# Moving a weight prefetch in time and in memory: three more weight tiles in the space of the raw inputs, most of them behind the last q/k/v loads, and hand-ordered first and last attention units

## The chip, the cores and the metric

The kernel runs on one core of one Trainium2 chip; the other cores do nothing. The engines go by their names in the profile: PE multiplies matrices (PEld loads its weights), DVE, ACT and POOL are the vector, scalar and GpSimd engines, SP issues the loads. "Products" are matmuls; acc is the PSUM buffer that takes those with a weight tile. The "DMA share" is the mean busy share of the core's 16 DMA engines; in short windows it reads a little above 1, so values near 1 mean full. The metric is the device time of one launch in microseconds. Two kernels are compared on the same chip in alternating rounds. "Span" is the time from the first to the last instruction of a profiled run; it is some 1.7 us shorter than the time of that run.

## The reference, cut to what matters

```python
# attention: 8 batches, 8 heads, 576 tokens, head dim 64
scores = q @ k^T / 8 + ALiBi bias; keys 0..127 tokens back only
x = softmax(scores) @ v                       # -> [8, 576, 512]
# spectral mixing
X = rfft(x, axis=1)[:, :64]                   # 64 modes
Y = X * (w_r + i w_i)                         # per mode a complex 512 x 512 matrix
u = x + irfft(Y)
out = u + relu(u @ w_ch)
```

The inputs q, k and v have 28.3 MB together. The weights w_r and w_i have 128 matrices of 512 x 512 in fp32, each 1.0486 MB: 134.2 MB. They are read once and nothing of them is used twice. The tolerance allows bf16 products.

## The kernel before

The kernel has three stages. Attention runs in 16 units (a batch and four heads), the weights stream past PE as tiles of 1 MB, and a tail of inverse transforms, ReLU and stores follows. The order of work on every engine is fixed by hand in this kernel. SP issues every load, also in a fixed order.

A cast frees a raw input buffer and at once asks for the load two units ahead:

```python
    def cast(self, u, w):
        src = self.loaded.pop((w, u))
        ...                                   # DVE casts to bf16
        self.load(w, u + 2)                   # raw pool: two buffers each of q, k, v
```

A weight tile is asked for every second stage, into a pool of eight buffers (`NW = 8`), among which is the one that first holds w_ch:

```python
        for stage in range(min(lags), n + max(lags)):          # n = 16 units
            for name, arg, lag in STAGE:                        # the software pipeline
                u = stage - lag
                if 0 <= u < n:
                    getattr(at, name)(u, arg)
            if stage > 0 and (stage % 2 == 1 or stage == n - 2):
                load_w()                                        # first call: w_ch
            if stage == 12:
                nc.gpsimd.tensor_copy(wch, wq[0])
```

In the weight stage every step uses one tile and asks for the next one. A load must wait until PE has used the tile whose buffer it takes:

```python
        for g in range(NM // 4):
            for i in range(8):
                w = wq[1 + 2 * m + ri]
                for a in range(4):
                    nc.tensor.matmul(acc[...], lhsT=XC[...], rhs=w[:, a]...)
                load_w()
                ...                           # side work: x @ w_ch, transposes
```

XC holds the spectra of all 16 units, so the first of these products needs the last unit of attention. Its last steps are two value products into one PSUM buffer (`av`), two norms on DVE, the spectrum on PE (`xt`) and its copy to XC by ACT.

The softmax here doesn't subtract the row's maximum and nothing guards it: scores larger than these inputs give would overflow.

## Time and profile before

| | before |
|---|---|
| median of the runs | 492.09 us before the change was run, 491.88 with one run more |
| profiled run | 487.15 us, span 485.5 us |
| DMA queue empty | about 128.5 to 139.5 us |
| first weight product (acc) | 137.0 us |
| last weight landed | about 439.7 us |
| last weight product to the end | 43.1 us |

The first fence shows four rows of the page of the kernel before: the span in 40 slices of 12.1 us, with busy tenths of PE and DVE, the DMA engines, and what they moved.

```profile
PE   1777767658579676675575667668678686688994
DVE  6599898989852101011011010211111201002885
...
DMA  8999999999549999999999999999999999992677
GB/s 252 315 285 269 320 286 327 291 288 259 234 171 423 421 421 420 422 422 420 421 422 422 421 423 421 421 421 421 422 419 423 423 421 420 422 422 98 241 277 263
```

Attention fills the first eleven slices, at about 285 GB/s on average. From slice 13 to 36 the weights stream at 421 GB/s, so that a tile takes 1.0486 MB / 421 GB/s = 2.49 us. PE is busy for two thirds of that time. The slices of 5 and 4 tenths, the eleventh and twelfth, are the thing to see: in about half of each DMA has nothing to do.

The next fence has the windows view of the kernel before. Columns: window, its length, then busy time and instructions of PE, PEld, DVE, ACT and POOL, granted clock, DMA share, GB/s.

```profile
120.00:124.00 4.00, 2.67 (x50) 1.87 (x48) 3.93 (x10) 4.00 (x6) 0.00 (x0) 1.00 0.88 343
124.00:128.00 4.00, 2.66 (x64) 2.29 (x61) 3.86 (x9) 3.70 (x6) 0.00 (x0) 1.00 1.01 424
128.00:132.00 4.00, 2.03 (x31) 1.64 (x32) 2.42 (x5) 0.00 (x0) 0.00 (x0) 0.61 0.04 14
132.00:136.00 4.00, 2.83 (x30) 2.40 (x27) 2.42 (x15) 0.00 (x0) 1.50 (x9) 0.50 0.00 0
136.00:140.00 4.00, 3.04 (x13) 1.21 (x12) 3.75 (x5) 0.87 (x2) 0.00 (x0) 0.50 0.07 8
```

Why it has nothing to do is seen in the timeline of SP, which issues the loads. These two lines follow each other:

```profile
119.89 0.38 SPq L386 DMA_DIRECT2D w<-in_moe_w_i_dram  x1
138.91 0.33 SPq L386 DMA_DIRECT2D w<-in_moe_w_r_dram  x1
```

All eight buffers are spoken for at 119.9 us, and their data is there at 128.5. The next load is issued at 138.9, when PE has used the first tile. From then on DMA never stops until the last weight has landed. The chain of waits shows this as long pieces of one kind (start, length, what):

```profile
168.80 18.74 DMA w<-in_moe_w_i_dram
187.58 1.08 PE acc L496 x4
188.68 18.75 DMA w<-in_moe_w_i_dram
```

Each piece is one load in the full queue of eight: 8 x 2.49 = 19.9 us from its issue to its product. So the time of this kernel is: when streaming can resume, plus the tiles still to come times 2.49, plus the tail.

### The profile page before, as it was taken

What the parts mean: (1) busy time and instruction counts of PE and PEld (TensorE: products, weight loads), DVE (VectorE), ACT (ScalarE), POOL (GpSimd) and SP (SyncE); (2) the same over time, 40 slices, a digit from 0 to 9 for tenths busy, and PEclk for the clock granted to TensorE, in tenths of its full rate; (3) what the DMA queues carried; (4) which work ended last, traced back from release to release, by engine and by line L of the source; (5) the groups of instructions that cost most, each with busy time, mean ns of one, the idle gap of its engine ahead of it and who ended that gap; (6) DMA issues with size and microseconds to landing.
All of it is one profiled execution on the core that took longest, in us unless ns stands there. A gap on an engine that the chain in (4) does not pass through costs nothing.

```text
span 485.5 us, 6274 instructions
## 1 busy us (share of the span) xinstructions
PE 339.8 (70%) x2411; PEld 175.5 (36%) x2430; DVE 189.4 (39%) x395; ACT 156.4 (32%) x212; POOL 33.5 (7%) x58
## 2 busy tenths in 40 slices
PE   1777767658579676675575667668678686688994
PEld 1455555546434323232232223323333232223431
DVE  6599898989852101011011010211111201002885
ACT  3897977988531000000000000101010100002674
POOL 6101000000010000000000000000000000000564
PEclk9997987998869989989989999988888978769999
DMA  8999999999549999999999999999999999992677
GB/s 252 315 285 269 320 286 327 291 288 259 234 171 423 421 421 420 422 422 420 421 422 422 421 423 421 421 421 421 422 419 423 423 421 420 422 422 98 241 277 263
DMA packets 71087, 173.44 MB, mean 357 GB/s; under 512 B 41360, under 2 KB 41360, under 8 KB 54672
## 3 DMA queue, kind: packets, MB, share of 16 engines
q1 hardware_dynamic: 71056, 173.03, 94.8%
q8 instruction: 19, 0.31, 0.3%
q14 instruction: 12, 0.10, 0.1%
HBM read 163.58 MB, written 9.44 MB: 356 GB/s over the span
## 4 chain that ended last, share of the span: by engine, by line
DMA 58%; PE 16%; DVE 14%; ACT 4%; issue 4%; SPq 3%; POOL 1%; POOLq 0%; DVEq 0%; ACTq 0%
DMA w<-in_moe_w_i_dram 45%; DMA w<-in_moe_w_r_dram 8%; PE acc L496 6%; DMA kr<-in_k_dram 4%; DVE x L296 3%; DVE att_130 L252 3%; DVE att_131 L252 2%; SPq L178 2%; DVE k L200 2%; DVE q L200 1%; PE av L282 1%; DMA qr<-in_q_dram 1%; PE warm L486 1%; PE mm L540 1%; PE mm L550 1%
## 5 line engine op out<-in xcount | busy, mean ns | idle before, releaser
L496 PE MATMUL acc<-w,XC 128*32 128x512 bf16 x512 | 153.3, 433 | 85.8 <-DMA w<-in_moe_w_r_dram 42.2
L496 PEld LDWEIGHTS <-XC 128*32 128x32 bf16 x512 | 64.7, 137 | 151.8 <-issue 125.8
L481 ACT CAST XW<-my 128x512 bf16<-128x512 f32 x36 | 21.1, 585 | 237.3 <-PE my L479 208.8
L475 DVE COPY xT<-tr 128x512 bf16<-128x512 bf16 x36 | 15.3, 425 | 161.8 <-PE tr L473 161.7
L563 POOL TENSOR_TENSOR r<-r,x 128x512 f32<-128x512 f32 x18 | 20.8, 1157 | 324.6 <-ACT r L560 324.6
L479 PE MATMUL my<-wch,xT 128*128 128x512 bf16 x129 | 38.6, 405 | 2.9 <-DVE xT L475 1.5
L240 ACT ACTIVATE att_130<-sc 128x1024 bf16<-128x1024 f32 x32 | 31.9, 1050 | 2.3 <-PE sc L231 2.2
L240 ACT ACTIVATE att_131<-sc 128x1024 bf16<-128x1024 f32 x32 | 32.1, 1038 | 0.5 <-PE sc L231 0.4
L427 DVE CAST yq<-acc 128x512 bf16<-128x512 f32 x16 | 11.0, 688 | 49.7 <-PE acc L496 49.7
L296 DVE TENSOR_TENSOR x<-av,rec 128x640 bf16<-128x640 f32 x32 | 26.4, 825 | 1.1
L569 DVE TENSOR_TENSOR o<-yy,r 128x512 f32<-128x512 f32 x36 | 23.6, 688 | 6.3 <-ACT r L560 4.3
L560 ACT ACTIVATE r<-mm 128x512 f32<-128x512 f32 x36 | 21.2, 597 | 8.9 <-PE mm L550 4.9
L252 DVE TENSOR_TENSOR att_131<-att_131,mask 128x1024 bf16<-128x1024 bf16 (+2 forms) x40 | 23.4, 618 | 0.0
L282 PEld LDWEIGHTS <-att_131 128*128 128x128 bf16 x288 | 12.9, 109 | 27.9 <-DVE x L296 25.5
L458 ACT CAST Zs<-zw 64x512 bf16<-64x512 f32 x16 | 9.2, 577 | 40.3 <-PE zw L449 40.1
L479 PEld LDWEIGHTS <-xT 128*128 128x128 bf16 x144 | 11.8, 102 | 28.6 <-issue 21.3
L215 ACT COPY qkT_128<-tp 128x1152 bf16<-128x1152 bf16 x15 | 16.8, 1117 | 15.9 <-PE tp L209 15.8
L252 DVE TENSOR_TENSOR att_130<-att_130,mask 128x1024 bf16<-128x1024 bf16 (+2 forms) x40 | 21.7, 576 | 0.3 <-ACT att_130 L240 0.3
L209 PE MATMUL tp<-ident,q 128*128 128x128 bf16 x144 | 14.0, 259 | 11.1 <-DVE q L200 7.8
L459 DVE CAST Zs<-z 64x512 bf16<-64x512 f32 x16 | 11.0, 687 | 22.5 <-PE z L452 22.3
L215 ACT COPY qkT_129<-tp 128x1152 bf16<-128x1152 bf16 x16 | 18.2, 1135 | 1.6 <-PE tp L209 1.6
L315 PE MATMUL xt<-F,x 128*128 128x128 bf16 x160 | 12.7, 246 | 4.7 <-DVE x L296 3.4
(95 smaller groups left out, 339.9 us busy)
## 6 DMA issues: line engine op xcount, KB each, us to landing
w<-in_moe_w_r_dram SPq DMA_DIRECT2D x64, 1024.0 KB, 18.7
w<-in_moe_w_i_dram SPq DMA_DIRECT2D x64, 1024.0 KB, 18.7
qr<-in_q_dram SPq DMA_DIRECT2D x16, 576.0 KB, 5.4
kr<-in_k_dram SPq DMA_DIRECT2D x16, 576.0 KB, 5.0
vr<-in_v_dram SPq DMA_DIRECT2D x64, 128.0 KB, 5.9
out_dram<-o SPq DMA_DIRECT2D x32, 256.0 KB, 2.4
vr<-in_v_dram SPq DMA_DIRECT2D x16, 64.0 KB, 5.2
w<-in_moe_w_ch_dram SPq DMA_DIRECT2D x1, 1024.0 KB, 8.5
```

Source lines behind the costliest of these rows:

```text
L215: (self.nc.vector.tensor_copy if (u, w) == (0, "q") else self.nc.scalar.copy)(dst.rearrange("q h (p j) -> q h p j", j=TPP), tp.rearrange(" ...
L240: self.nc.scalar.activation(self.att[u % 2][:, kt * 8 * P : (kt + 1) * 8 * P], sc.rearrange("p e n -> p (e n)"), AF.Exp, scale=1.0 / math. ...
L252: nc.vector.tensor_tensor(out=heads[:, :, c0 : c0 + n], in0=heads[:, :, c0 : c0 + n], in1=mask[:, :, m0 : m0 + n], op=ALU.mult,)
L282: nc.tensor.matmul(dst, lhsT=lhsT, rhs=vb[:, kt, hv, : D + 1], start=(n == 0), stop=(n == len(terms) - 1),)
L296: nc.vector.tensor_tensor(out=self.x[:, b, :, cs].rearrange("p t (h d) -> p h t d", h=2), in0=tiles[:, :, :, :D], in1=rec.unsqueeze(-1).br ...
L475: nc.vector.tensor_copy(xT, tr)
L479: nc.tensor.matmul(mm, lhsT=xT[:, dt], rhs=wch[:, dt], start=(dt == 0), stop=(dt == 3))
L481: nc.scalar.copy(XW[:, i], mm)
L496: nc.tensor.matmul(acc[32 * (i // 2) : 32 * (i // 2) + 32], lhsT=XC[:, c0 : c0 + 31 * NM + 1 : NM], rhs=w[:, a].bitcast(BF16)[:, 1::2], st ...
L560: nc.scalar.activation(r, mm, AF.Relu)
L563: nc.gpsimd.tensor_tensor(out=r, in0=r, in1=xi, op=ALU.add)
L569: nc.vector.tensor_tensor(out=o, in0=yy, in1=r, op=ALU.add)
```

## The change

Its intent is to give DMA more tiles to load before PE frees the first one, and to end attention earlier.

1. Three extra weight tiles lie in the memory of the raw q/k/v buffers once these are done, so that eleven tiles can be loaded before PE frees one. They are used once; the depth in the stream stays eight.
2. Of the eight ordinary tiles only four are loaded among the q/k/v loads, and four behind them. w_ch comes in two halves through raw q buffers and is copied by ACT instead of POOL.
3. The first units are ordered by hand: loads q0, k0, q1, k1 first, the table of sines in two parts, 24 products to warm PE.
4. In the last unit, the second value product takes another PSUM buffer, and ACT and DVE share the copy of `xt`.
5. Some buffers of the tail (Zs, r, o) move to the memory of the extra tiles.

```diff
-            if stage > 0 and (stage % 2 == 1 or stage == n - 2):
+            if stage in (3, 6, 9, 12):
                 load_w()
-            if stage == 12:
-                nc.gpsimd.tensor_copy(wch, wq[0])
+            if stage == n - 4:
+                halves = [at.raw.tile([P, 2, TPP, D], FP32, tag="qr", name="wch") for _ in "ab"]
+                ...                                        # two DMAs of w_ch
+            if stage in (n - 3, n - 2):
+                load_w(2)
+            if stage == n - 1:
+                for a, t in enumerate(halves):
+                    nc.scalar.copy(wch[:, 2 * a : 2 * a + 2], t.rearrange(...))
+                at.rawctx.close()
+                wpool2 = w2ctx.enter_context(
+                    tc.tile_pool(name="w2", bufs=3, side="right", reuse_waits="tile"))
+                load_w(3, wpool2)
...
-        for w in "qkv":
-            for u in range(2):
-                at.load(w, u)
+        for w, u in (("q", 0), ("k", 0), ("q", 1), ("k", 1), ("v", 0), ("v", 1)):
+            at.load(w, u)
...
+            for _ in range(24):
+                nc.tensor.matmul(wt, lhsT=ident, rhs=ident, start=True, stop=True)
+            run("cast", "q", 0)
+            run("transpose", "q", 0)
...                                                        # and so on for k0, q1, k1
-        av = self.ps.tile([P, 2, 512], FP32, tag="av")
+        last = u == len(self.units) - 1 and e == 1
+        av = self.ps.tile([P, 2, 512], FP32, tag="sc" if last else "av", ...)
...
+            lo, hi = slice(0, 2), slice(2, 4)              # last unit only
+            nc.scalar.copy(view[:, lo, 8 + b : 24 : 8, :], xt[:, 0, lo])
+            nc.vector.tensor_copy(view[:, hi, 8 + b : 24 : 8, :], xt[:, 1, hi])
...
+                if 8 * g + i == 16:
+                    w2ctx.close()
+                    right = mctx.enter_context(tc.tile_pool(name="late", ...))
+                    Zs = right.tile([P, B, 2, DM], BF16, name="Zs")
```

More of the change, by code (lines that the diff above doesn't have):

```diff
@@ L80, in _forward_table @@
         nc.vector.tensor_scalar_add(ang[:, :, ri, :], prod, float(S) / (4 - 2 * ri))
+    yield
     _sin_of(nc, pool, F[:, : FULL + 1].rearrange("p a b -> p (a b)"),
@@ L133, in __init__ @@
         self.units = [(b, g) for b in range(B) for g in range(self.NG)]
-        self.raw = ctx.enter_context(tc.tile_pool(name="raw", bufs=2))
+        self.rawctx = ctx.enter_context(ExitStack())
+        self.raw = self.rawctx.enter_context(tc.tile_pool(name="raw", bufs=2, side="right"))
         self.mid = ctx.enter_context(tc.tile_pool(name="amid", bufs=2))
@@ L206, in transpose @@
         src = self.casted.pop((u, w))
-        tp = self.ps.tile([P, TPP, P], BF16, tag="tp")
+        if (u, w) == (0, "k"):
+            tp = self.ps.tile([P, TPP, P], BF16, tag="sc", bufs=2, name="tp")
+        else:
+            tp = self.ps.tile([P, TPP, P], BF16, tag="tp", name="tp")
         for j in range(TPP):
@@ L214, in evacuate @@
         dst = self.qkT[u % 2][:, "qk".index(w), :, : self.S]
-        (self.nc.vector.tensor_copy if (u, w) == (0, "q") else self.nc.scalar.copy)(
+        (self.nc.vector.tensor_copy if u < 2 and w == "q" else self.nc.scalar.copy)(
             dst.rearrange("q h (p j) -> q h p j", j=TPP),
@@ L263, in value @@
         att, vb = self.att[u % 2], self.vb[u % 3]
-        av = self.ps.tile([P, 2, 512], FP32, tag="av")
+        last = u == len(self.units) - 1 and e == 1
+        av = self.ps.tile([P, 2, 512], FP32, tag="sc" if last else "av", bufs=2 if last else 1)
         for h in range(2):
@@ L311, in spectrum @@
         NM = self.F.shape[2] // 2
-        xt = self.ps.tile([P, 4, 2, NM], FP32, tag="tp")
+        last = u == len(self.units) - 1
+        xt = self.ps.tile([P, 2, 4, 2, NM], FP32, tag="tp")
         for a in range(4):
@@ L315, in spectrum @@
                 nc.tensor.matmul(
-                    xt[:, a].rearrange("p r m -> p (r m)"),
+                    xt[:, a // 2 if last else 0, a].rearrange("p r m -> p (r m)"),
                     lhsT=self.x[:, b, st, a::4],
@@ L331, in channels @@
         view = self.XC[:, : 4 * NC * NM].rearrange("p (a c m) -> p a c m", a=4, c=NC)
-        nc.scalar.copy(view[:, :, 8 + b : 24 : 8, :], xt)
-        nc.scalar.mul(view[:, :, b, :], xt[:, :, 1, :], -1.0)
+        if u < len(self.units) - 1:
+            nc.scalar.copy(view[:, :, 8 + b : 24 : 8, :], xt[:, 0])
+            nc.scalar.mul(view[:, :, b, :], xt[:, 0, :, 1, :], -1.0)
+        else:
+            lo, hi = slice(0, 2), slice(2, 4)
+            nc.scalar.copy(view[:, lo, 8 + b : 24 : 8, :], xt[:, 0, lo])
+            nc.scalar.mul(view[:, lo, b, :], xt[:, 0, lo, 1, :], -1.0)
+            nc.vector.tensor_copy(view[:, hi, 8 + b : 24 : 8, :], xt[:, 1, hi])
+            nc.vector.tensor_scalar_mul(view[:, hi, b, :], xt[:, 1, hi, 1, :], -1.0)
 @with_exitstack
@@ L361, with load_w @@
     wch = const.tile([P, 4, DM], BF16, name="wch")
-    with tc.tile_pool(name="setup", bufs=1) as pool:
-        make_identity(nc, ident)
-        kv_i = pool.tile([P, 2], I32)
-        nc.gpsimd.iota(kv_i, [[-P, 2]], base=0, channel_multiplier=1)
-        kv = pool.tile([P, 2], FP32)
-        nc.vector.tensor_copy(kv, kv_i)
-        _forward_table(nc, pool, F, S)
-        for h in range(H):
-            slope = 2.0 ** (-8.0 * (h + 1) / H)
-            nc.scalar.activation(ek[:, h], kv, AF.Exp, scale=slope)
     wpool = ctx.enter_context(tc.tile_pool(name="w", bufs=NW))
     wq = []
-    def load_w():
-        i = len(wq) - 1
-        if i >= 2 * NM:
-            return
-        t = wpool.tile([P, 4, DM], FP32, tag="w", name="w")
-        if i < 0:
-            src = moe_w_ch.rearrange("(a p) e -> p a e", p=P)
-        else:
+    def load_w(n=1, wpool=wpool):
+        for i in range(len(wq), min(len(wq) + n, 2 * NM)):
+            t = wpool.tile([P, 4, DM], FP32, tag="w", name="w")
             src = (moe_w_r, moe_w_i)[i % 2][i // 2].rearrange("(p a) e -> p a e", a=4)
-        nc.sync.dma_start(out=t, in_=src)
-        wq.append(t)
+            nc.sync.dma_start(out=t, in_=src)
+            wq.append(t)
+    w2ctx = ExitStack()
     with ExitStack() as actx:
@@ L391, with run @@
         n = len(at.units)
-        for w in "qkv":
-            for u in range(2):
-                at.load(w, u)
+        for w, u in (("q", 0), ("k", 0), ("q", 1), ("k", 1), ("v", 0), ("v", 1)):
+            at.load(w, u)
+        done = set()
+        def run(name, arg, u):
+            if 0 <= u < n and (name, arg, u) not in done:
+                done.add((name, arg, u))
+                getattr(at, name)(u, arg)
+        make_identity(nc, ident)
+        with tc.tile_pool(name="setup", bufs=1) as pool:
+            kv_i = pool.tile([P, 2], I32)
+            nc.gpsimd.iota(kv_i, [[-P, 2]], base=0, channel_multiplier=1)
+            kv = pool.tile([P, 2], FP32)
+            nc.vector.tensor_copy(kv, kv_i)
+            table = _forward_table(nc, pool, F, S)
+            next(table)
+            wt = at.ps.tile([P, P], FP32, tag="av", bufs=1, name="warm")
+            for _ in range(24):
+                nc.tensor.matmul(wt, lhsT=ident, rhs=ident, start=True, stop=True)
+            run("cast", "q", 0)
+            run("transpose", "q", 0)
+            next(table, None)
+            run("cast", "k", 0)
+            run("transpose", "k", 0)
+            run("evacuate", "q", 0)
+            run("evacuate", "k", 0)
+            for h in range(H):
+                slope = 2.0 ** (-8.0 * (h + 1) / H)
+                nc.scalar.activation(ek[:, h], kv, AF.Exp, scale=slope)
         at.fixtures()
@@ L398 @@
         nc.gpsimd.memset(XC[:, 4 * NC * NM :], 0.0)
+        for name, arg, u in (("cast", "q", 1), ("cast", "k", 1), ("transpose", "q", 1),
+                             ("evacuate", "q", 1)):
+            run(name, arg, u)
         lags = [lag for _, _, lag in STAGE]
@@ L401 @@
             for name, arg, lag in STAGE:
-                u = stage - lag
-                if 0 <= u < n:
-                    getattr(at, name)(u, arg)
-            if stage > 0 and (stage % 2 == 1 or stage == n - 2):
+                run(name, arg, stage - lag)
+            if stage in (3, 6, 9, 12):
                 load_w()
-            if stage == 12:
-                nc.gpsimd.tensor_copy(wch, wq[0])
+            if stage == n - 4:
+                halves = [at.raw.tile([P, 2, TPP, D], FP32, tag="qr", name="wch") for _ in "ab"]
+                halves = [t.rearrange("p e j d -> p (e j d)")[:, : 2 * DM] for t in halves]
+                for a, t in enumerate(halves):
+                    nc.sync.dma_start(
+                        out=t.rearrange("p (a e) -> p a e", a=2),
+                        in_=moe_w_ch[2 * a * P : 2 * a * P + 2 * P].rearrange(
+                            "(a p) e -> p a e", p=P),
+                    )
+            if stage in (n - 3, n - 2):
+                load_w(2)
+            if stage == n - 1:
+                for a, t in enumerate(halves):
+                    nc.scalar.copy(wch[:, 2 * a : 2 * a + 2], t.rearrange("p (a e) -> p a e", a=2))
+                at.rawctx.close()
+                wpool2 = w2ctx.enter_context(
+                    tc.tile_pool(name="w2", bufs=3, side="right", reuse_waits="tile")
+                )
+                load_w(3, wpool2)
     with ExitStack() as mctx:
@@ L413 @@
         YT = fix.tile([P, 2, 4, B, 2, HM], BF16, name="YT")
-        Zs = fix.tile([P, B, 2, DM], BF16, name="Zs")
         with tc.tile_pool(name="setup2", bufs=1) as pool:
@@ L421 @@
         XW = big.tile([P, 9 * (B // 2), DM], BF16, name="XW")
-        load_w()
         def quad_end(acc, g):
@@ L488 @@
         quads, side, todo = [], [], 0
+        Zs = None
         for g in range(NM // 4):
@@ L492 @@
                 m, ri = 4 * g + i // 2, i % 2
-                w = wq[1 + 2 * m + ri]
+                w = wq[2 * m + ri]
                 for a in range(4):
@@ L503 @@
                 load_w()
+                if 8 * g + i == 16:
+                    w2ctx.close()
+                    right = mctx.enter_context(
+                        tc.tile_pool(name="late", bufs=1, side="right", reuse_waits="tile")
+                    )
+                    Zs = right.tile([P, B, 2, DM], BF16, name="Zs")
                 if quads:
@@ L558, in end @@
             inverse(mm, 0, bs, st, False)
-            r = pool.tile([P, DM], FP32, tag="r", bufs=3)
+            r = right.tile([P, DM], FP32, tag="r", bufs=3, name="r")
             nc.scalar.activation(r, mm, AF.Relu)
@@ L567, in store @@
             xi, bs, st = tiles[i]
-            o = pool.tile([P, DM], FP32, tag="o", bufs=5)
+            o = right.tile([P, DM], FP32, tag="o", bufs=5)
             nc.vector.tensor_tensor(out=o, in0=yy, in1=r, op=ALU.add)
```

## The prediction

> **What bounds the kernel now.** (1) Attention, 0 to 134 us: windows give DVE 3.9 us busy of most 4 us and a DMA share of 0.9 to 1.15, so both are near their limit, at only about 285 GB/s, because v arrives in 256 B runs (the Trainium skill, "DMA: Bandwidth & Descriptors", Specifications, puts line rate at 512 B or more; the trace agrees: 421 in the weight stage). (2) Weight streaming, 139.5 to 440 us: DMA share 1.01 at 421 GB/s throughout, PE busy two thirds; the chain of waits is almost only "DMA w". A tile of 1.0486 MB takes 2.49 us. (3) Tail, 45 us. Total time is when streaming resumes, plus the tiles left times 2.49, plus the tail.
>
> Before streaming lies a hole: windows show a DMA share of 0.09, 0.00, 0.00, 0.13 from 128 to 140 us. All eight weight buffers are full at 128.5, and PE frees the first at 138.9: 11 us.
>
> **What the change does.**
> - Three extra weight tiles in the raw inputs' memory: eleven load before PE frees one, 117 remain instead of 120: 3 x 2.49 = 7.5 us of the hole is filled. Later the depth is eight again; the gain is kept as DMA stays saturated.
> - Fewer weights among q/k/v loads: before the last k load 3 tiles instead of 5 (w_ch counted), 5 us of DMA time; before the last v load 5 instead of 6. DVE's waits for kr (6.5 us, 5 times, just after weight tiles) shrink to 2 to 3. Attention ends some 4 us earlier; DVE work of 6.6 us a unit limits more.
> - Last unit: the second value product takes another PSUM buffer instead of waiting for the norm (1.2 us), and ACT and DVE share the copy of xt (ACT took 0.58+0.39): 1 to 1.5 us.
> - First unit: q and k first, table split, 24 warming products. DVE's 5.0 us wait for the third q remains, as the same loads precede it: 0 to 1 us.
> - wch moves from POOL (1.96 us) to two ACT copies when ACT is idle; same bytes.
>
> **On the critical path.** First acc product moves from 137 to about 132. DMA, with three tiles more to load by then, would end at about 136, less what it stalls less: the hole closes nearly wholly. DMA then bounds 2 to 427 us without a break; the gain is the hole, 11 us, plus 1 of stalls, not the sum of the parts. Last weight lands at about 428 instead of 440, tail unchanged. Profile span 485.5 to about 473.5; the median of 492.1 becomes 480, range 476 to 484. Faster by over 2% (below 482.2): 0.75; within 2%: 0.24; slower: 0.01.
>
> **What would show it.** DMA row without the slices of 5 and 4 tenths; windows of 126 to 140 with DMA share near 1; first acc at 131 to 134; kr waits below 3 us; waits for w in the same 18 us pieces; tail within 1 us.
>
> **What would make it wrong.** Attention bound by DVE so that it ends no earlier, leaving 3 us of hole (gain 8); the extra loads issued late, behind the ACT copies of wch and the last v cast; late Zs and output buffers delaying the tail; PE at half clock freeing the first buffers late; or a DMA with more slack in attention than its share shows (gain over 14).

## The result, and the profile after

The changed kernel took 478.56 us in the median of 4 runs (477.9 to 479.33), against 491.88 for 4 runs of the kernel before (490.33 to 494.97). The ratio is 0.9722, with a 95% interval of 0.9673 to 0.9772. Here and below a ratio is the mean time of one kernel's runs over that of the other's of the same rounds, so it is not quite the ratio of the medians. Executions over 1.5% slower than the fastest of the same kernel are left out of the means. Later, on chip 11, the same pair gave 479.7 us and 0.9793 (0.976 to 0.9825). The change is faster by 2.1 to 2.8%; that it is faster is clear in both sessions, that it is faster by over 2% only in the first (the second interval takes in 0.98).

The same rows of the page after:

```profile
PE   4587675767669968667766867766776676588994
DVE  6699998989651210101101011111121211003885
...
DMA  8999999999999999999999999999999999991687
GB/s 254 313 280 262 314 301 250 336 226 303 399 419 414 407 421 420 420 422 422 420 423 419 422 423 422 420 423 420 420 423 420 423 420 421 423 417 50 241 281 253
```

The slices of 5 and 4 tenths are gone, and the stream of weights begins two slices sooner. The windows of the changed kernel show it closer, in the columns that were explained above:

```profile
120.00:124.00 4.00, 2.18 (x55) 1.80 (x52) 3.72 (x8) 4.00 (x6) 0.00 (x0) 1.00 0.99 412
124.00:128.00 4.00, 2.39 (x36) 2.04 (x36) 3.07 (x8) 1.09 (x2) 0.41 (x1) 0.54 1.01 426
128.00:132.00 4.00, 2.33 (x20) 2.06 (x20) 1.28 (x4) 0.55 (x2) 0.94 (x9) 0.50 1.02 428
132.00:136.00 4.00, 3.80 (x15) 1.46 (x16) 3.67 (x17) 0.00 (x0) 0.00 (x0) 0.50 1.02 422
136.00:140.00 4.00, 2.16 (x8) 0.59 (x5) 1.41 (x2) 2.44 (x2) 0.00 (x0) 0.75 1.03 426
```

PE does no more in these 20 us than before, but DMA moves at full rate through all of them. The timeline of SP tells from what. The last of the ordinary tiles, the three extra ones, and the first tile that had to wait for PE:

```profile
120.58 0.43 SPq L385 DMA_DIRECT2D w<-in_moe_w_i_dram  x1
125.12 0.33 SPq L385 DMA_DIRECT2D w<-in_moe_w_r_dram  x1
125.63 0.33 SPq L385 DMA_DIRECT2D w<-in_moe_w_i_dram  x1
126.01 0.43 SPq L385 DMA_DIRECT2D w<-in_moe_w_r_dram  x1
134.12 0.33 SPq L385 DMA_DIRECT2D w<-in_moe_w_i_dram  x1
```

SP waited 4.0 us for ACT to copy w_ch out of the raw buffers before it could issue the first extra tile. DMA did not notice, since four ordinary tiles had just been queued.

For all traces I worked out two numbers. "Idle" is the sum over the half-microsecond windows from 118 to 150 us of one less the DMA share, where the share is under 1. Some 0.7 us of this is left even where DMA never stops. "Landed" is the start of the first half microsecond at the end of the stream in which the DMA share is below one half, plus that share of it. "Work" is landed less idle: the time in which DMA was busy, or idle elsewhere (before 118 us too).

| kernel (trace) | first acc product | first load that waited for PE | idle | landed | work |
|---|---|---|---|---|---|
| before | 137.0 | 138.9 | 13.6 | 439.7 | 426.1 |
| before, second trace | 139.0 | 140.9 | 12.7 | 442.1 | 429.5 |
| changed | 132.2 | 134.1 | 2.0 | 429.6 | 427.6 |
| changed, second trace | 133.6 | 135.5 | 2.1 | 431.7 | 429.5 |

The work of the two kernels overlaps, and idle differs by 11 us. The change did not make DMA do its work faster; it took away the time in which it had none. From the start of the last acc product to the end, both kernels take 43.1 us (42.9 and 43.1 in the second traces). But this last product comes 2.7 and 2.1 us after the last weight has landed in the kernel before, and 3.5 and 4.0 us after it in the changed one. In between PE works without a pause, as 24 products named "warm" stand between those of the last tiles. So of the 10 us by which the last weight lands sooner, the spans show 9.3 and 8.3 us.

### The profile page after: what moved, and what is told of

It reads as the page before. It is cut to its first block, busy times and chain, and to the rows that moved or that the text cites. A ratio compares the mean times of both kernels' runs of the same rounds, so it can differ in the third digit from the quotient of the medians.

```text
span 476.2 us, 6345 instructions
## 1 busy us (share of the span) xinstructions
PE 342.8 (72%) x2454; PEld 174.1 (37%) x2454; DVE 189.2 (40%) x398; ACT 157.3 (33%) x213; POOL 29.2 (6%) x57
## 4 chain that ended last, share of the span: by engine, by line
DMA 56%; PE 18%; DVE 17%; ACT 4%; issue 2%; SPq 1%; POOL 0%; POOLq 0%; DVEq 0%; ACTq 0%
DMA w<-in_moe_w_i_dram 50%; PE acc L541 7%; DVE x L302 3%; DVE att_88 L257 3%; DMA vr<-in_v_dram 3%; DVE att_87 L257 2%; DMA kr<-in_k_dram 2%; DVE k L202 2%; DMA qr<-in_q_dram 2%; PE my L523 2%; DVE q L202 2%; PE warm L530 1%; PE mm L591 1%; PE mm L601 1%; PE av L288 1%
## 5 line engine op out<-in xcount | busy, mean ns | idle before, releaser
L541 PEld LDWEIGHTS <-XC 128*32 128x32 bf16 x512 | 63.6, 138 | 145.0 <-issue 119.4
L519 DVE COPY xT<-tr 128x512 bf16<-128x512 bf16 x36 | 15.3, 425 | 159.6 <-PE tr L517 159.5
L523 PE MATMUL my<-wch,xT 128*128 128x512 bf16 x144 | 43.1, 429 | 3.2 <-DVE xT L519 3.2
L257 DVE TENSOR_TENSOR att_88<-att_88,mask 128x1024 bf16<-128x1024 bf16 (+2 forms) x40 | 21.7, 576 | 0.0
L257 DVE TENSOR_TENSOR att_87<-att_87,mask 128x1024 bf16<-128x1024 bf16 (+2 forms) x40 | 21.7, 576 | 0.0
L220 ACT COPY qkT_85<-tp 128x1152 bf16<-128x1152 bf16 x15 | 16.8, 1117 | 9.8 <-PE tp L214 9.7
L220 ACT COPY qkT_86<-tp 128x1152 bf16<-128x1152 bf16 x15 | 17.0, 1130 | 2.0 <-PE tp L214 1.9
```

The source lines that it names most:

```text
L220: (self.nc.vector.tensor_copy if u < 2 and w == "q" else self.nc.scalar.copy)(dst.rearrange("q h (p j) -> q h p j", j=TPP), tp.rearrange(" ...
L257: nc.vector.tensor_tensor(out=heads[:, :, c0 : c0 + n], in0=heads[:, :, c0 : c0 + n], in1=mask[:, :, m0 : m0 + n], op=ALU.mult,)
L523: nc.tensor.matmul(mm, lhsT=xT[:, dt], rhs=wch[:, dt], start=(dt == 0), stop=(dt == 3))
L541: nc.tensor.matmul(acc[32 * (i // 2) : 32 * (i // 2) + 32], lhsT=XC[:, c0 : c0 + 31 * NM + 1 : NM], rhs=w[:, a].bitcast(BF16)[:, 1::2], st ...
```

## The experiments

Theory A, from the prediction: the time is set by when the last weight lands, and what counts is only DMA's idle time ahead of the stream. Rival B: each part of the change is worth its own length, whatever the others do. All twelve runs gave the reference's result within tolerance. Times below are medians; ratios are against the kernel before on the same chip and in the same rounds. The last three columns are of one profiled run, which need not be typical: that of e5 took 480.31 us and that of e2 481.77, the fastest of their sets, that of e8 485.14, and that of e9 479.58, the slowest of its set.

| run | what | median us | ratio (95%) | first acc | idle | landed |
|---|---|---|---|---|---|---|
| changed | | 478.56 / 479.7 | 0.9722 / 0.9793 | 132.2 / 133.6 | 2.0 / 2.1 | 429.6 / 431.7 |
| e1_no_extra | no extra tiles | 484.96 | 0.9885 (0.9857 to 0.9914) | 133.1 | 7.4 | 437.2 |
| e7_one_extra | one extra tile | 483.72 | 0.9856 (0.9807 to 0.9904) | 132.6 | 5.4 | 434.7 |
| e5_depth_only | extra tiles alone | 483.58 | 0.9851 (0.9818 to 0.9885) | 136.9 | 4.6 | 432.2 |
| e2_early_w | weights among the loads | 483.96 | 0.9854 (0.9828 to 0.9881) | 135.6 | 4.1 | 432.7 |
| e8_early_pool | the same, earlier release | 483.43 | 0.9877 (0.9836 to 0.9919) | 138.2 | 5.5 | 436.1 |
| e6_late_w | all weights behind the loads | 477.45 / 477.15 | 0.9728 / 0.9734 | 125.7 / 125.6 | 0.7 / 0.9 | 428.6 / 428.2 |
| e9_late_delay | the same, 5 us of delay | 477.26 | 0.9742 (0.9708 to 0.9777) | 131.6 | 0.8 | 431.2 |
| e3_first_undone | first units as before | 479.35 | 0.978 (0.9727 to 0.9832) | 132.9 | 1.8 | 431.2 |
| e4_last_undone | last unit as before | 477.38 | 0.9748 (0.9705 to 0.9791) | 133.4 | 1.7 | 429.7 |
| before_again | kernel before | 488.49 | 0.9949 (0.989 to 1.0008) | 139.0 | 12.7 | 442.1 |

### The depth

```diff
-                load_w(3, wpool2)
+                load_w(0, wpool2)        # e1_no_extra;  load_w(1, wpool2): e7_one_extra
```

> The changed kernel without the three extra weight tiles (eight buffers only). Theory A (only the DMA hole counts): DMA has loaded all inputs and eight tiles by about 129 us, and PE frees the first buffer at 134.1 as in the changed kernel, so a hole of 5 to 6.5 us opens and the time rises by that: 483.5 to 485. Rival B (the parts are worth their full size whatever the others do; depth is worth 3 x 2.49 us): +7.5, about 486. Rival C (the depth is worth nothing, the gain comes from a faster attention): within 1 us of 478.6.

> The changed kernel with one extra weight tile instead of three (nine before the first is freed). Theory A: DMA would run dry at about 131.7 and resumes at about 134.8: hole of 3 to 4 us: 481.5 to 482.6; with none (the earlier run) 2.5 us more. Rival B: two tiles less cost 5.0 us: 483.6.

Without the extra tiles the hole comes back. Windows of e1_no_extra:

```profile
124.00:128.00 4.00, 2.42 (x54) 1.94 (x54) 3.36 (x8) 2.77 (x3) 0.00 (x0) 0.94 1.00 422
128.00:132.00 4.00, 2.34 (x21) 2.06 (x20) 1.66 (x4) 0.18 (x1) 1.38 (x9) 0.50 0.70 295
132.00:136.00 4.00, 2.87 (x10) 1.20 (x12) 3.29 (x17) 0.38 (x2) 0.00 (x0) 0.50 0.02 6
136.00:140.00 4.00, 2.53 (x12) 0.82 (x8) 2.08 (x2) 1.77 (x2) 0.00 (x0) 0.78 0.86 336
```

DMA runs dry at 130.5 us and resumes at 136. Idle grows by 5.4 us (2.0 to 7.4), and the median by 6.4 us against the first of the changed kernel, by 5.3 against the second. That is Theory A's number; but as the two ratios of the changed kernel differ, anything from 4.5 to 8 us can be read from the ratios, so that rival B's 7.5 is not excluded. Rival C, that depth is worth nothing, is.

With one extra tile idle is 3.4 us above that of the changed kernel, as expected, but the median of 483.72 is 1 us above Theory A's range, on rival B's 483.6, and only 1.2 us better than with none. The sizes between none and three are not resolved well: the intervals overlap, and the two ran on different chips.

The extra tiles alone, with everything else as near to the kernel before as the new memory layout allows:

```diff
-            if stage in (3, 6, 9, 12):
+            if stage in (1, 3, 5, 7, 9, 11, 13, 14):
                 load_w()
-            if stage in (n - 3, n - 2):
-                load_w(2)
...                       # and the edits of e3_first_undone and e4_last_undone, below
```

> The three extra tiles alone: the weight tiles in attention at about the old places (one in stages 1, 3, 5, 7, 9, 11, 13, 14), first and last units in the old order. Theory A: PE frees the first buffer at about 139.5 as before, DMA has work until 136.7, so a hole of about 3 us is left: 481 to 482.5. Rival B: it lacks the 4.8 us by which attention became shorter: about 483.5. Rival D (the DMA total is fixed and depth alone closes all of it): within 1 us of 478.6.

The median was 483.58 us, outside the 481 to 482.5 of Theory A and on rival B's 483.5. In its trace the extra tiles were issued only at 129.8 us, later than foreseen; the next run shows the same and looks closer.

### The place of the weights

e2_early_w moves only the weights back among the q/k/v loads (the first edit above).

> The changed kernel with its weight tiles put back among the q/k/v loads (one in stages 1, 3, 5, 7, 9, 11, 13, 14), everything else kept. Attention ends later, first acc product at 135 to 136.5 instead of 132.2, and DVE waits for kr go back to 5 to 7 us. Theory A: DMA's work reaches to 136.7, so a hole of 0 to 1.5 us: 478.5 to 480. Rival B: the 3 to 4 us of attention are paid in full: 481.5 to 482.5.

It took 483.96 us, 4.3 to 5.4 us more than the changed kernel (3 to 6.5 by the ratios). That is a miss for Theory A's number, and above rival B's too. DVE's waits for k were 4.8 us, against 3.0 in the changed kernel. Windows of e2_early_w:

```profile
124.00:128.00 4.00, 1.91 (x50) 1.54 (x47) 3.93 (x9) 3.91 (x7) 0.00 (x0) 1.00 1.00 422
128.00:130.00 2.00, 1.62 (x26) 1.44 (x27) 1.18 (x4) 0.83 (x1) 0.00 (x0) 0.57 0.43 66
130.00:132.00 2.00, 0.83 (x15) 0.67 (x13) 1.90 (x5) 0.00 (x0) 0.96 (x5) 0.50 0.72 283
...
138.00:140.00 2.00, 2.00 (x14) 0.85 (x10) 1.93 (x3) 0.00 (x0) 0.00 (x0) 0.87 0.72 201
```

There are two gaps. The second, at 138, is the old kind: PE frees the first buffer at 137.5 instead of 134.1, because attention is longer. The first, at 128, I had not foreseen: the extra tiles are issued at 128.9 only, when the raw memory comes free, and with the ordinary tiles loaded early DMA has nothing queued behind which to hide that wait. In the changed kernel the four late tiles do just that.

Which of the two gaps costs? e8_early_pool frees the raw memory sooner:

```diff
-                    nc.scalar.copy(wch[:, 2 * a : 2 * a + 2], ...)
+                    nc.gpsimd.tensor_copy(wch[:, 2 * a : 2 * a + 2], ...)
```

> The early-weights kernel (one in stages 1, 3, 5, 7, 9, 11, 13, 14), with wch copied out by the idle POOL instead of ACT, so that the raw inputs' memory is free for the extra tiles sooner: they are issued at 122 to 125 us instead of 128.9, and DMA's gap of 2.3 us at 128 to 131 closes. Theory A1 (the late issue of the extra tiles is what costs): 2 us faster than the early-weights kernel, 0.9854 of before becomes about 0.981. Theory A2 (what costs is that PE frees the first buffer only at 137.5, as attention is longer): the gap just moves to 136 to 138, the time stays within 0.7 us.

Windows of e8_early_pool:

```profile
128.00:130.00 2.00, 0.99 (x28) 0.70 (x22) 1.97 (x5) 2.00 (x3) 0.00 (x0) 1.00 1.01 414
...
136.00:138.00 2.00, 0.82 (x8) 0.55 (x6) 0.56 (x3) 0.55 (x2) 0.00 (x0) 0.50 0.33 135
138.00:140.00 2.00, 1.83 (x6) 0.80 (x8) 1.77 (x14) 0.00 (x0) 0.00 (x0) 0.50 0.05 12
```

The gap at 128 is closed and a gap at 136 to 141 has opened; the ratio is 0.9877 where 0.981 would have been a gain. So A1 falls and A2 fits: when attention is too long, DMA has to wait for PE to free the first buffer, and in these two runs it did not matter at which moment it waited. They ran on different chips, and part of the size of this gap is that attention itself was 2.6 us longer in this trace than in that of e2_early_w; whether the copies on POOL had a part in that was not tested.

Now the other way: all eight ordinary tiles behind the q/k/v loads.

```diff
-            if stage in (3, 6, 9, 12):
-                load_w()
             if stage in (n - 3, n - 2):
-                load_w(2)
+                load_w(4)
```

> The changed kernel with none of its weight tiles among the loads of attention: all eight in the last but two and last but one stages, then the three extra. Attention gets shorter, first acc product at 126 to 130. Theory A: DMA is what ends last, its total is the same and every stall of it in attention is now lost: 478.5 to 481, never faster. Rival B: faster by what attention gains: 474 to 476.

Attention is now 6.5 us shorter than in the changed kernel: first acc product at 125.7 us. The time is 477.45 us, between the ranges of both theories: Theory A had said "never faster" and 478.5 at best, rival B 474 to 476. It came at a ratio of 0.9728 where the changed kernel had 0.9722 in another session. So it was run again beside the changed kernel.

> The changed kernel once more, on the same chip as the three that follow, so that they can be compared directly: ratio to before 0.968 to 0.976.

> The late-weights kernel once more, beside the changed kernel. Its trace had 0.7 us of DMA idle between 118 and 150 us where the changed kernel had 2.0, while its attention ended 6.5 us earlier. Theory A (only DMA's idle time counts): 0 to 1.5 us faster than the changed kernel. Rival B (a shorter attention is worth its length): 4 to 6 us faster.

On the same chip the changed kernel took 479.7 us (478.81 to 481.21, six runs; its ratio of 0.9793 is outside the expected 0.968 to 0.976), this one 477.15 (475.41 to 478.48, six runs). No run of the one overlaps with the other, so it is faster by about 2.5 us (by the ratios 2.9). That is less than half of the 8 us by which attention is shorter in these two traces (133.6 to 125.6), and 1 us more than Theory A allowed. In these two traces 1.2 us of it is idle (2.1 against 0.9), and 2.2 is work (429.5 against 427.3). The work varies nearly as much between two traces of the changed kernel (427.6 and 429.5), so where the second part comes from stays open.

What early weights do to attention is best seen in one line of the windows view, from 20 to 100 us. Kernel before:

```profile
20.00:100.00 80.00, 58.26 (x902) 44.17 (x902) 74.33 (x145) 68.37 (x77) 1.96 (x1) 0.89 1.05 302
```

The changed kernel:

```profile
20.00:100.00 80.00, 56.34 (x940) 42.38 (x936) 76.87 (x154) 70.70 (x79) 0.00 (x0) 0.90 1.06 289
```

All weights behind the loads (second trace):

```profile
20.00:100.00 80.00, 54.96 (x982) 41.48 (x984) 79.14 (x159) 73.89 (x82) 0.00 (x0) 1.00 1.05 275
```

The third pair counts DVE's work. Without weights DVE is busy for 79.1 of 80 us and gets through 159 instructions instead of 145: attention runs at DVE's pace. The granted clock differs too (0.89, 0.90, 1.00), but e4_last_undone, with weights as in the changed kernel, had 0.98 and 153 instructions of DVE, so the clock is not what does it. The DMA share is 1.05 or 1.06 in all three, so it does not say whether DMA or DVE was the limit; the waits of DVE for q, k and v do: 11.8 us in the whole of the kernel before, 9.2 in the changed one, 4.1 here. The Trainium skill warns of this: "Perfetto Trace Analysis", section Identifying the Most-Contended Engine, calls occupancy misleading for the DMA engines. But the low 275 GB/s is no sign of slack either: had DMA had time to spare in attention, loading less there would have lost it, and the last weight would have landed later than in the changed kernel. It landed at 428.2 and 428.6 us, against 429.6 and 431.7. The three lines agree: in these 80 us the kernels issue five, three and no weight tiles (w_ch counted). If each takes its 2.49 us, an estimate from these lines, q, k and v come at 280, 275 and 275 GB/s in the time that is left, so each early tile takes its time from them.

### A delay on the chain that should cost nothing

The sharpest test of Theory A is to lengthen attention where it has slack. e9_late_delay is e6_late_w with the last norm written seven times over, with the same result:

```diff
-        nc.vector.tensor_tensor(out=self.x[...], in0=..., in1=rec..., op=ALU.mult)
+        for _ in range(7 if u == len(self.units) - 1 and e == 1 else 1):
+            nc.vector.tensor_tensor(out=self.x[...], in0=..., in1=rec..., op=ALU.mult)
```

> The late-weights kernel, with the last norm on DVE written seven times instead of once: 6 x 0.825 = 4.95 us of useless work on the chain from the last unit to the first acc product, no DMA touched, same result. First acc product moves from 125.7 to about 130.7, first buffer free from 127.7 to about 132.6. Theory A: DMA's queue reaches to 136.7, nothing is lost: within 0.7 us of the late-weights kernel. Rival B: 4.5 to 5 us slower.

The timeline of e9_late_delay shows the delay, and its windows show that DMA goes on:

```profile
121.88 5.97 DVE L303 TENSOR_TENSOR x<-av,rec 128x640 bf16<-128x640 f32 x7
```

```profile
124.00:128.00 4.00, 0.09 (x1) 0.09 (x2) 3.83 (x6) 0.00 (x0) 0.00 (x0) 0.50 1.02 424
128.00:132.00 4.00, 2.66 (x22) 2.17 (x23) 1.23 (x7) 0.55 (x2) 0.00 (x0) 0.50 1.00 418
132.00:136.00 4.00, 4.00 (x17) 1.55 (x16) 3.75 (x12) 0.00 (x0) 0.00 (x0) 0.50 1.03 426
```

PE stands still for most of 124 to 128 us and the first acc product slips from 125.6 to 131.6 (5.1 us by the delay, the rest since attention itself was later in this trace). The median is 477.26 us against 477.15 without the delay, on the same chip and in the same rounds. Rival B wanted 4.5 to 5 us. Theory A holds: 5 us of work on the chain to the first product cost nothing that is seen (0.1 us by the medians, 0.4 by the ratios, 0.8 by the means of all six runs; the spread of the runs would hide up to about 2), as DMA's queue reached past it. The table's 431.2 for "landed" is of the slowest of the six runs (479.58 us); the difference lies outside the 118 to 150 us of "idle", some 2 us of it as idle time before 118 us.

### The hand-ordered units

```diff
-        for w, u in (("q", 0), ("k", 0), ("q", 1), ("k", 1), ("v", 0), ("v", 1)):
+        for w, u in (("q", 0), ("q", 1), ("k", 0), ("k", 1), ("v", 0), ("v", 1)):
...                      # e3: no warming products, table in one piece, no hand order,
...                      #     the second q copied by ACT
-        last = u == len(self.units) - 1 and e == 1
+        last = False    # e4: old PSUM buffer, xt copied by ACT alone
```

> The changed kernel with the old order of the first units (loads q q k k v v, the table in one piece, no warming products, no hand order, the second q copied out by ACT). Theory A: the third q lands at the same time, DMA's total is the same: within 0.7 us of the changed kernel's 478.6, and the windows of 120 to 140 us show DMA share near 1. Rival B: the hand order at the start is worth 1 us or more: 479.6 to 481.

> The changed kernel with the old last unit (second value product in its old PSUM buffer, xt copied out by ACT alone). First acc product at 133.2 to 133.8 instead of 132.2; first buffer free at about 135.3. Theory A: DMA still has work until 136.7, so the time stays within 0.7 us of 478.6. Rival B: it is on the critical path and costs its 1 to 1.5 us: 479.6 to 480.1.

Without the hand order of the first units the median was 479.35 us, with runs from 476.7 to 483.75, between the two medians of the changed kernel, and between Theory A's range and rival B's. Without that of the last unit it was 477.38. The last unit's order does shorten its chain: from the start of the last value products to the first acc product it takes 7.2 us in both traces of the changed kernel, and 8.2 us in e4 and in the kernel before. But this is inside DMA's queue, and rival B's 479.6 for its loss was not seen. No effect of either is seen; with intervals of 2.6 and 2.1 us to each side, one of 1 to 2 us could not be.

### Why the kernel before spreads so widely

> The kernel before, unchanged, for a second trace: the first trace was of a run of 487.15 us, while the timed runs were 490.3 to 495.0. If the difference lies in the hole before streaming (its length depends on when PE frees the first buffers), a trace of a longer run has a longer hole (11.2 us in the first trace) by as much as the span is longer than 485.5; if in the tail, the tail is longer than 45.9 us; if in neither, attention is longer.

The four runs took 486.51 to 494.3 us, the last of them slow. The second trace, of a run of 488.78 us, has a span of 487.1 us instead of 485.5, the first acc product at 139.0 instead of 137.0, and hardly a different idle. So the difference is in attention, whose DMA work took longer with the same bytes, and neither in the hole nor in the tail. What makes it vary from run to run was not found.

## Why the prediction was right

- **The number.** The predicted fall of 12 us (492.1 to 480) lies between the two measured, 13.3 and 10.1 us. In the traces the span fell by 9.3 us, to 476.2 where 473.5 was predicted, and by 8.3 in the second pair; the first trace before was of a run of 487.15 us, shorter than all the timed ones of its session. So the mechanism below is right, and that the median came within 1.5 us of 480 was in part luck.
- **The hole is what the change removes.** Right. Idle ahead of the stream fell by 11.6 us (13.6 to 2.0); the prediction put the hole at 11. The last weight landed at 429.6 us (predicted 428), the first acc product came at 132.2 (predicted 131 to 134).
- **Three tiles are worth 7.5 us of it.** Right in mechanism, near in size: taking them away cost 5.3 to 6.4 us. Alone (e5_depth_only) they gave 490.4 x (1 - 0.9851) = 7.3 us.
- **Attention ends some 4 us earlier, and 1 to 1.5 us come from the last unit.** Right: 4.8 us in sum at the first acc product (5.4 in the second traces), of which 1.0 for the last unit.
- **The gain is the hole and not the sum of the parts.** Right, but shown only beyond the change. With 490.4 us for the kernel before (its median beside these runs), depth alone gave 7.3 us, all but depth (e1_no_extra) 490.4 x (1 - 0.9885) = 5.6 us, and both together 10.2 and 13.6 by the same reckoning. As the sum is hardly larger than the hole, these numbers would fit rival B as well. The cap is seen where attention is made shorter still (8 us, worth 2.5 to 3) and longer again (5 us, worth 0.1 to 0.8).
- **Plus 1 us of stalls in attention.** Not seen. DMA's work was 427.6 us in one trace of the changed kernel and 429.5 in the other, against 426.1 and 429.5 before. This term was within the noise and should have been left out.
- **DVE's waits for k shrink to 2 to 3 us; the wait of 5 us for the third q remains.** The waits for k went from 6.5 to 3.0 us. The third q cost 3.8 us instead of 5.0, and some waits moved to other q tiles and to v: waits for q, k and v together are 9.2 us instead of 11.8 (9.5 instead of 15.3 in the second traces).
- **The tail is unchanged.** Right from the last acc product on: 43.1 us in both. From the last weight's landing it is 46.6 and 47.1 us instead of 45.8 and 45.0, as told above. So the spans add up: 11.6 us less idle, 1.5 more work and 0.8 more here make the 9.3 of the first pair; 10.6, 0 and 2.1 make the second, within rounding.
- **The risk that the extra loads are issued late, behind the copies of w_ch.** They are, by 4.0 us, and it costs nothing here, because the four late tiles lie in front of them. The prediction saw the late weights only as a relief for attention and missed this second use.

- **What bounds attention.** The prediction had DMA and DVE both near their limit there. That holds, but its sign for DMA, a share near 1, was not evidence (see the lines from 20 to 100 us).

The bound by DMA in the stream was read with the help of the Trainium skill. "HBM Reference", section Specifications (TRN2), says that a core streaming alone measures about 425 GB/s; the stream here had 421. "DMA: Bandwidth & Descriptors", section Specifications, wants transfers of at least 512 B for line rate; q, k and v, with v in runs of 256 B, came at 275 GB/s when nothing else was loaded. No run changed the length of these runs, so that they are the cause of the lower rate was argued and not shown.

## What to carry to other kernels

Where a stream from memory bounds the kernel, look for the time in which its queue is empty, and compare two moments: when DMA has filled every buffer, and when the consumer frees the first. Here moving these two together gave the gain; once they had met, time saved ahead of the consumer was worth little (8 us gave 2.5 to 3), and a delay test showed the slack. Memory that comes free late can hold more prefetch; in the changed kernel other loads, queued in front of it, covered the wait for it. What that cover is worth was not measured: where it was missing, closing the gap gained nothing (e8_early_pool).

## What the Trainium skill lacked or had wrong

- "DMA: Bandwidth & Descriptors", section Why small descriptors are slow, reckons an overhead of 27% for a descriptor of 256 B, from the first of the two mechanisms that it names; for the second it gives no loss of speed, and so none in all. Here q, k and v in equal parts, alone on the queue, moved at 275 GB/s. If q and k, in runs of 2304 B, had the stream's 421 GB/s, an estimate for v from these two numbers is 1 / (3/275 - 2/421) = 162 GB/s, a loss of 62%. It is a lower bound for the speed of v if DMA had slack that the runs did not show, and q and k were not measured apart.
- The same page says nothing of how far the time of such loads varies: DMA's work up to the last weight (idle before 118 us included) took 426.1 and 429.5 us in two traces of the same kernel, and 426.1 to 430.7 in the fourteen of this case, with almost the same bytes.
- "Perfetto Trace Analysis", section Identifying the Most-Contended Engine, wants HBM utilization in place of occupancy, and then sends the reader to find which DMA resource binds. In attention 275 to 302 GB/s against the stream's 421 look like a third of slack, and by the argument above there was none to be had; neither of the two measures told by itself, so that second step is the one that counts.
- The same page, section Optimization Strategy, says that performance may be improved by interleaving regimes whose most-contended engine differs. It says nothing of regimes that share one. Here DMA was near its limit in both, and weight tiles among the q/k/v loads were slower than behind them: 483.96 us against 477.45 on the same chip.
